# The sixth down step of the last two tiles by seven block products, new places for its left sides, and a third place for weight sums

## The chip, the cores and the metric

The kernel runs on one core of a Trainium2 chip. The time is that of one execution on the device in microseconds (us), and less is better. Five engines work side by side, each through its own queue in order: TensorE (PE, matrix products, with PEld for the loads of its stationary side), VectorE (DVE), ScalarE (ACT), GpSimd (POOL) and SyncE (SP), which here does nothing but issue transfers between the chip's two memories: the device memory, and the on-chip memory in which the engines read and write. An instruction at the head of a queue that waits for another engine or for a transfer holds up all that stands behind it in that queue.

## The reference: what is computed

An input `x` of 4096 rows by 640 columns goes through two blocks, each added to its input. The first is a spectral filter (Fourier transforms, a small network on the frequencies, and back); it is not touched. The second is a gated network:

```python
h = _layernorm(x, axis=-1) * (1 + cb) + sb
x = x + gb * ((_silu(h @ w_gate) * (h @ w_up)) @ w_down)
```

`w_gate` and `w_up` are 640 by 1728, `w_down` is 1728 by 640. The last product, here called the down product, is where the change lies. All of it is asked for in 32-bit precision. The kernel gets there with a faster number format of TensorE: each operand is split into a high and a low part, and a product is three matmuls (high by high, high by low, low by high).

## The kernel before, in words

The 4096 rows are worked as 32 blocks of 128 rows, in six tiles: tiles 0 and 1 of four blocks, tiles 2 to 5 of six. For each tile the 1728 inner columns come in chunks of 128, two chunks to a pair. A pair p (0 to 5) has a step for the gate (`g`), a step for `w_up` (`u`) and a down step. Behind the gate step of pair p+1 stands the down step of pair p; behind the sixth `u` step stands a step `m` (chunk 12, gate and up together), and then the sixth down step, which also takes chunk 12 and the half-filled chunk 13. The step `s`, early in the tile, makes chunk 13.

In tiles 2 to 5 the gate and up steps are done by Strassen's scheme in Winograd's form: a product of matrices of two by two blocks with seven block products instead of eight, from sums and differences of the blocks. The sums of weight blocks (`wt`) are made once in tiles 0 and 1, stored in the device memory (`td`) and loaded two per step in tiles 2 to 5 (line 2206). In each step PE makes seven products into four banks (lines 1887 to 1889, and 1898 to 1900 for the fifth block of rows), ACT copies four partial results out (`s_x`, `s_v`, `s_y`, `s_z`, line 1906), PE goes on adding into the same banks once the copy is made, and DVE adds copy and bank (line 1913).

The down product is plain in tiles 0 to 3 (`down`, line 2142, chunk 12 at line 2152): 11 matmuls of 320 columns for each of the tile's blocks and halves in a sixth step. In tiles 4 and 5 its first five steps are done by seven products too (`down7`, line 2056). This needs the seven blocks and sums of `w_down` per pair, split into high and low: `block_sums` (lines 1311 to 1350) loads four blocks (`B11` to `B22`), makes T1 to T4 on POOL, the high part on ACT (line 1328), the low part on DVE (line 1331), and stores them in `wsd` (line 1334); that runs beside tiles 1 and 2, and before tile 4 begins all of these stores must have been issued (the loop `until(("wst", p, x))`). `block_loads` brings them back. And it needs the left sides: `lefts` (line 1797) makes the products of gate and up (A11 to A22) and the sums S1 to S4 on POOL, and splits them on ACT (line 1816) and DVE (line 1819). In `down7` the seven products go into three groups of banks, X, Y and Z; X takes four of the seven products, with a DVE addition into the rows of `x` after each (line 2038); Z is copied by ACT and added by POOL.

In the sixth down step the weights of pairs 5 and 6 (6 is chunks 12 and 13) are loaded unsplit (`wdr`) and split in each tile by ACT (line 1373) and DVE (line 1377).

Beside the tile at hand runs the row work for the next one: the spectral result of each row block is finished, normed, transposed, and its left sides are split and stored (`hs<-ho`, lines 1465 to 1591), using the places `pc`, `px`, `h32` and `ho`.

The order of every queue is fixed when the program is built. A planner walks through the matmuls, keeps modelled times for each engine and each place (`room`), and puts a step of a chain into the queues when its inputs and places are free by that model (`tries`). What is needed and not yet placed is forced (`until`, `force`). The number of places per name stands in `bufs`: two for `wt`, two for `e` (where a split weight block waits for its store).

## Time and profile before

| what | value |
|---|---|
| median of 3 runs | 1481.1 us |
| the runs | 1473.35, 1481.52, 1481.1 us |
| profiled execution | 1476.28 us, of which the profile's span is 1474.4 us |
| PE busy | 1421.5 us, 96% |
| DVE, ACT, POOL busy | 1091.5, 805.4, 539.5 us |
| mean granted clock of TensorE | 0.996 |
| first matmul of tile 4 | 1083.9 us after the span's start |

The page gives the busy time of each engine and splits the span into 40 slices. From about 325 us on, when the gated network begins, PE is at nine tenths or more in every slice, and only the few microseconds in which it is not can be won without taking matmuls away. Busy times overlap: a matmul of 320 columns takes 312 ns from start to end, but the next starts some 147 ns after it.

### The profile page before, as it was taken

What the parts mean: (1) busy time and instruction counts of PE and PEld (TensorE: products, weight loads), DVE (VectorE), ACT (ScalarE), POOL (GpSimd) and SP (SyncE); (2) the same over time, 40 slices, a digit from 0 to 9 for tenths busy, and PEclk for the clock granted to TensorE, in tenths of its full rate; (3) what the DMA queues carried; (4) which work ended last, traced back from release to release, by engine and by line L of the source; (5) the groups of instructions that cost most, each with busy time, mean ns of one, the idle gap of its engine ahead of it and who ended that gap; (6) DMA issues with size and microseconds to landing.
All of it is one profiled execution on the core that took longest, in us unless ns stands there. A gap on an engine that the chain in (4) does not pass through costs nothing.

```text
span 1474.4 us, 24146 instructions
## 1 busy us (share of the span) xinstructions
PE 1421.5 (96%) x8646; PEld 1343.8 (91%) x8646; DVE 1091.5 (74%) x1979; ACT 805.4 (55%) x1594; POOL 539.5 (37%) x648
## 2 busy tenths in 40 slices
PE   6999999997999999999999999999999999999999
PEld 2799999975888888899999999999999999999998
DVE  8478888878788688848878857777747767467774
ACT  6578989845445565545565545555524435244432
POOL 5400110034564353412445422443324544046541
PEclk9999999999999999999999999999999999999999
DMA  9946555738767988798878995766796566965542
GB/s 376 334 166 182 157 187 163 221 104 273 256 246 236 367 290 273 271 390 293 276 271 264 319 373 189 260 223 205 268 363 205 202 209 206 374 196 208 202 156 100
DMA packets 171784, 363.21 MB, mean 246 GB/s; under 512 B 21457, under 2 KB 91537, under 8 KB 169617
## 3 DMA queue, kind: packets, MB, share of 16 engines
q1 hardware_dynamic: 163152, 344.14, 68.0%
q0 software_dynamic: 6928, 14.91, 3.2%
q10 hardware_dynamic: 1584, 2.62, 0.5%
q8 instruction: 68, 1.11, 0.3%
q14 instruction: 52, 0.42, 0.1%
HBM read 254.34 MB, written 98.11 MB: 239 GB/s over the span
## 4 chain that ended last, share of the span: by engine, by line
PE 70%; DVE 13%; DMA 8%; ACT 4%; issue 3%; POOL 1%; SPq 1%; DVEq 0%; ACTq 0%; POOLq 0%
PE pd L2142 16%; PE pw L1887 7%; PE pw L1888 7%; PE pw L1889 7%; PE pd_X L2056 4%; PE pc L657 2%; PE pg L1752 2%; PE pg L1753 2%; PE pg L1754 2%; PE pw L1898 2%; PE pw L1900 2%; PE pw L1899 2%; DVE wb L1222 2%; DMA wt<-td 2%; PE pd_Y L2056 2%
## 5 line engine op out<-in xcount | busy, mean ns | idle before, releaser
L2142 PE MATMUL pd<-wdh,a 128*128 128x320 f32 x1192 | 276.6, 312 | 2.0 <-DVE a L1789 1.8
L2142 PEld LDWEIGHTS pd<-wdh,a 128*128 128x128 f32 x1192 | 204.2, 190 | 3.0 <-DVE a L1789 2.1
L2142 PE MATMUL pd<-wdl,a 128*128 128x320 f32 x628 | 194.4, 311 | 0.0
L1222 DVE TENSOR_TENSOR wb<-r,wb 128x512 fp32r<-128x512 f32 (+3 forms) x156 | 161.8, 1043 | 21.1 <-ACT wb L1219 19.1
L2114 DVE TENSOR_TENSOR x<-x,pd 128x320 f32<-128x320 f32 x264 | 120.6, 479 | 55.1 <-PE pd L2142 50.3
L1887 PE MATMUL pw<-h,wt 128*128 128x384 f32 x416 | 140.5, 338 | 7.0 <-DMA wt<-td 5.2
L1888 PE MATMUL pw<-h,wt 128*128 128x384 f32 x416 | 139.2, 335 | 0.0
L1889 PE MATMUL pw<-h,wt 128*128 128x384 f32 x416 | 139.2, 335 | 0.0
L1219 ACT ACTIVATE wb<-r 128x512 fp32r<-128x512 f32 (+3 forms) x172 | 118.1, 703 | 32.9 <-PE pw L1900 22.7
L2142 PEld LDWEIGHTS pd<-wdl,a 128*128 128x128 f32 x628 | 119.0, 189 | 0.5
L1887 PE MATMUL pw<-h,wb 128*128 128x384 f32 x312 | 104.9, 336 | 0.0
L1889 PE MATMUL pw<-h,wb 128*128 128x384 f32 x312 | 104.7, 336 | 0.1
L1888 PE MATMUL pw<-h,wb 128*128 128x384 f32 x312 | 104.6, 335 | 0.0
L1752 PE MATMUL pg<-ht,wb 128*128 128x512 f32 x260 | 102.9, 396 | 1.2 <-ACT wb L1219 1.2
L1754 PE MATMUL pg<-ht,wb 128*128 128x512 f32 x260 | 101.8, 391 | 2.2 <-DVE wb L1222 2.2
L1753 PE MATMUL pg<-ht,wb 128*128 128x512 f32 x260 | 101.6, 391 | 0.0
L1465 POOL TENSOR_TENSOR cr<-cr,gab 128x640 f32<-128x640 f32 x28 | 46.9, 1676 | 126.8 <-DMA cr<-s 87.4
L1887 PEld LDWEIGHTS pw<-h,wt 128*128 128x128 f32 x416 | 78.1, 188 | 9.6 <-DMA wt<-td 5.1
L714 POOL DMA_DIRECT2D s<-co x28 | 15.5, 552 | 192.9 <-ACT co L713 186.1
L1906 ACT ACTIVATE s_x<-pw 128x384 f32<-128x384 f32 x52 | 25.4, 489 | 100.8 <-PE pw L1889 100.2
L1888 PEld LDWEIGHTS pw<-h,wt 128*128 128x128 f32 x416 | 78.2, 188 | 0.0
L1889 PEld LDWEIGHTS pw<-h,wt 128*128 128x128 f32 x416 | 78.2, 188 | 0.0
(315 smaller groups left out, 3977.7 us busy)
## 6 DMA issues: line engine op xcount, KB each, us to landing
wt<-td SPq DMA_DIRECT2D x104, 512.0 KB, 5.3
hs<-ho SPq DMA_DIRECT2D x52, 512.0 KB, 4.9
h<-hs SPq DMA_DIRECT2D x32, 768.0 KB, 7.6
r<-in_B_w_gate_dram SPq DMA_DIRECT2D x36, 640.0 KB, 5.6
r<-in_B_w_up_dram SPq DMA_DIRECT2D x36, 640.0 KB, 5.3
wdr<-wdd SPq DMA_DIRECT2D x25, 640.0 KB, 4.5
td<-wt SPq DMA_DIRECT2D x25, 512.0 KB, 5.9
g<-s SPq DMA_DIRECT2D x28, 320.0 KB, 7.8
```

What stands on the lines that cost most here:

```text
L1219: act.activation(wbs[t, n][:, 0, ks, e], raw[t, n][:, ks, e], AF.Copy)
L1222: (pool if onp else dve).tensor_tensor(wbs[t, n][:, 1, ks, e], raw[t, n][:, ks, e], f32(wbs[t, n][:, 0, ks, e]), op=OP.subtract)
L1465: pool.tensor_tensor(crs[r], crs[r], gab, op=OP.mult)
L1752: mm(b, wh, hh, start=(kk == 0), stop=False)
L1753: mm(b, wh, hl, start=False, stop=False)
L1754: mm(b, wl, hh, start=False, stop=(kk == 4))
L1887: mm(b, w(0, kp), a[:, kp, 0], start=start and kp == 0, stop=False, skip_group_check=not start)
L1888: mm(b, w(0, kp), a[:, kp, 1], start=False, stop=False, skip_group_check=not start)
L1889: mm(b, w(1, kp), a[:, kp, 0], start=False, stop=kp == 1, skip_group_check=not start)
L2056: mm(bk[b, i][:, :320], l[ln][:, x, c], w[wn, y], start=new and j == 0, stop=j == 2, skip_group_check=not new)
L2114: dve.tensor_tensor(x2[:, e], x2[:, e], x[0][:, :320], op=OP.add)
L2142: mm(pd[g, hf][0][:, :320], l, m, start=i == 0, stop=i == len(s) - 1 and not (last and len(gs) > 1))
```

## The change

1. The sixth down step of tiles 4 and 5 is done by seven products as well (`down7` with `last`). Chunks 12 and 13 are added to the Y, Z and X banks in plain form (5 matmuls), and to a fourth group of banks V. Z is here added by DVE like the others.
2. `block_sums` therefore runs for pair 5 (seven blocks) and for pair 6 (four blocks, only split, `TB`). The weights of pair 6 are loaded into `px` and `h32`, places that the row work has left. The splits of `wdr` go from tiles 4 and 5.
3. `e` has one place instead of two; the sources of the left sides now lie in `pc` instead of `m`, S2 and S3 in `ho` instead of `e`.
4. `wt` has three places, used in turn.

```diff
-            bufs = {"R": 2, "h1": 1, "wb": 2, "wt": 2, "wd": 1, "wdh": 2, "wdl": 2, "pc": 4, "px": 2, "gt": 2, "ho": 2,
-                    "h32": 1, "sg": 4, "s": 5, "gx": 2, "rb0": 1, "rb1": 1, "ra0": 1, "ra1": 1, "m": 5, "e": 2}
+            bufs = {"R": 2, "h1": 1, "wb": 2, "wt": 3, "wd": 1, "wdh": 2, "wdl": 2, "pc": 4, "px": 2, "gt": 2, "ho": 2,
+                    "h32": 1, "sg": 4, "s": 5, "gx": 2, "rb0": 1, "rb1": 1, "ra0": 1, "ra1": 1, "m": 5, "e": 1}
...
             def take(tag, shape, dt, bufs, name):
+                if tag == "wt":
+                    turns[0] += 1
+                    if turns[0] % 3 == 0:
+                        return low_p.tile(shape, dt, tag=tag, name=name)
+                    bufs = 2
...
+                if p == NPR:
+                    def tail(hl, f):
+                        w = wds.setdefault((t, p), {})
+                        if hl:
+                            w[hl, f] = take("px", [P, D], F32R, 2, f"tl{t}_{f}")
+                            nc.sync.dma_start(f32(w[hl, f]), wsd[p, :, 1, 2 * f:2 * f + 2])
+                        else:
+                            v = take("h32", [P, 2, D], F32R, 1, f"th{t}")
...
+            TB = ("B11", "B12", "B21", "B22")
...
-                for x in ("B22", "B21", "B11", "T3", "T1", "T2", "T4"):
+                bl = TB if p == NPR else ("B22", "B21", "B11", "T3", "T1", "T2", "T4")
+                for x in bl:
...
-                if t in DT and p < NPR - 1:
+                if t in DT:
                     return block_loads(t, p)
...
-            LT = {"A11": "a0", "A12": "a1", "S1": "a2", "A22": "a3", "S2": "e", "S3": "e", "S4": "wd"}
+            LT = {"A11": "a0", "A12": "a1", "S1": "a2", "A22": "a3", "S2": "ho", "S3": "ho", "S4": "wd"}
...
+                    for b, ln, wn, a, hf in (("X", "A11", "B11", 0, 0), ("Y", "S1", "T1", 1, 1), ("X", "S2", "T2", 0, 1),
+                                             ("X", "S3", "T3", 1, 1)):
+                        for i in range(H):
+                            put(b, i, prod(ln, wn, i))
+                            read(b, i, a, hf, False)
+                        if b == "Y":
+                            for a in range(2):
+                                until(("act", t, 12, a))
+                    for i in range(H):
+                        put("Y", i, prod("S4", "B22", i), (0, 1))
+                        read("Y", i, 0, 1, True)
+                    for i in range(H):
+                        put("Z", i, prod("A12", "B21", i), (0, 0))
+                        read("Z", i, 0, 0, True)
+                        out(0, i)
+                    for i in range(H):
+                        fin = t == NT - 1 and i == H - 1
+                        put("X", i, prod("A22", "T4", i), (1, 0))
+                        read("X", i, 1, 0, True)
...
+                        put("V", i, (), (1, 1))
+                        read("V", i, 1, 1, True)
...
             def down(t, p):
-                if t in DT and p < NPR - 1:
+                if t in DT:
                     return down7(t, p)
...
-            for p in range(NPR - 1):
+            for p in range(NPR + 1):
                 down_s.add(block_sums(p))
...
                 if t == min(DT):
-                    for p in range(NPR - 1):
-                        for x in BL:
+                    for p in range(NPR + 1):
+                        for x in TB if p == NPR else BL:
                             until(("wst", p, x))
```

Where the order of instructions moves, in rows of the two programs (line, operation, what is written and read, shape; `x2`, `x3` counts equal rows that follow each other; a name carries step and number).

SP at the end of tile 3 and the start of tile 4. The `out_dram` rows bring the finished rows of tile 3 out, `hs<-ho` are left sides of tile 5, `wt_10` and `wt_11` are weight sums of tile 4's second step, `x_4_0` and `x_4_1` the rows to which tile 4's first down step adds. Before:

```order
L2128 DMA out_dram<-x_3_0_10007 128x640 x3
L2128 DMA out_dram<-x_3_1_10087 128x640 x2
L1591 DMA hs<-ho_2_2_12401 128x2x512
L1303 DMA wdh_0_0_12435<-wsd 128x1280
L1591 DMA hs<-ho_2_3_12422 128x2x512
L1669 DMA x_4_0_12464<-x2d 128x1920
L2206 DMA wt_10_12475<-td 128x1024
L2206 DMA wt_11_12498<-td 128x1024
L2128 DMA out_dram<-x_3_1_10087 128x640
L1303 DMA wdl_0_0_12531<-wsd 128x1280
L1669 DMA x_4_1_12536<-x2d 128x1920
```

Of the change, first where tile 4 starts:

```order
L2220 DMA out_dram<-x_3_0_10045 128x640 x3
L2220 DMA out_dram<-x_3_1_10074 128x640 x2
L1616 DMA hs<-ho_2_2_12459 128x2x512
L1359 DMA wsd<-B12hl_12134 256x1x320
L1359 DMA wsd<-B21hl_12487 256x1x320
L1359 DMA wsd<-B22hl_12491 256x1x320
L2298 DMA wt_11_12576<-td 128x1024
L2298 DMA wt_30_12584<-td 128x1024
L1616 DMA hs<-ho_2_3_12480 128x2x512
```

and then, seven rows further, up to tile 4's first down step:

```order
L1208 DMA r_5_12720<-in_B_w_gate_dram 128x5x256
L1694 DMA x_4_0_12758<-x2d 128x1920
L2220 DMA out_dram<-x_3_1_10074 128x640
L2298 DMA wt_41_12797<-td 128x1024
L2298 DMA wt_50_12825<-td 128x1024
L1694 DMA x_4_1_12831<-x2d 128x1920
```

Three stores of pair 6's split blocks now stand at the start of tile 4, ahead of `wt_11`, `wt_30` and the last `hs`; `wt_10` went ahead into tile 3; the loads of `x_4_0` and `x_4_1` moved back behind the loads of the third gate step.

ACT at the same place, where `s_0_x` is the copy of tile 4's first product. Before:

```order
L1583 ACTIVATE ho_2_2_12401<-sa_2_0_12211 128x2x128 x2
L1583 ACTIVATE ho_2_3_12422<-sa_2_1_12212 128x2x128 x2
L1906 ACTIVATE s_0_x<-pw_0_0_12428 128x384
L1906 ACTIVATE s_0_v<-pw_0_3_12439 128x384
L1920 ACTIVATE sg_0_00_12460<-s_0_x 128x384
```

and of the change:

```order
L1608 ACTIVATE ho_2_2_12459<-sa_2_0_12269 128x2x128 x2
L1608 ACTIVATE ho_2_3_12480<-sa_2_1_12270 128x2x128 x2
L1353 ACTIVATE B21hl_12487<-B_6_12022 128x320
L1353 ACTIVATE B22hl_12491<-B_6_11997 128x320
L1932 ACTIVATE s_0_x<-pw_0_0_12495 128x384
L1932 ACTIVATE s_0_v<-pw_0_3_12504 128x384
L1932 ACTIVATE s_0_y<-pw_0_0_12495 128x384
```

Two splits of pair 6 now stand ahead of the first copy of tile 4; with one place `e`, each may start only when the store of the block before it has landed.

DVE at the start of tile 4's sixth down step. `s_13_z` and `s_13_v` are the last sums of step `m`, `a_13_..` the low parts of chunk 12, `wb_1` the low part of a weight of tile 5, and `pd_5_X`, `pd_5_Y` the banks. Of the change:

```order
L1939 TENSOR_TENSOR s_13_v<-pw_13_0_14291,s_13_v 128x384
L2068 TENSOR_TENSOR x_4_0_12758<-x_4_0_12758,pd_5_X_14413 128x320
L1229 TENSOR_TENSOR wb_1_14418<-r_1_14145,wb_1_14418 128x512
L2068 TENSOR_TENSOR x_4_0_12758<-x_4_0_12758,pd_5_X_14427 128x320
L2068 TENSOR_TENSOR x_4_0_12758<-x_4_0_12758,pd_5_X_14435 128x320
L2068 TENSOR_TENSOR x_4_1_12831<-x_4_1_12831,pd_5_Y_14440 128x320
L2068 TENSOR_TENSOR x_4_1_12831<-x_4_1_12831,pd_5_Y_14446 128x320
L2068 TENSOR_TENSOR x_4_1_12831<-x_4_1_12831,pd_5_Y_14451 128x320
L1963 TENSOR_TENSOR a_13_01_14407<-sg_13_00_14343,a_13_01_14407 128x384
L1963 TENSOR_TENSOR a_13_11_14412<-sg_13_10_14381,a_13_11_14412 128x384
L2068 TENSOR_TENSOR x_4_0_12758<-x_4_0_12758,pd_5_X_14413 128x320
L2068 TENSOR_TENSOR x_4_0_12758<-x_4_0_12758,pd_5_X_14427 128x320
```

Before, no bank of the down step was read there until chunk 12's matmuls were done; now six additions and half of `wb_1` stand ahead of `a_13_..`, and the second reading of X behind it.

More of the change, by code (lines that the diff above doesn't have):

```diff
@@ L2028, in read @@
                     q = bk[b, i]
-                    if b == "Z":
+                    if b == "Z" and not last:
                         hold("s")
@@ L2041, in read, with put @@
                         room[f"p{tags[b, i]}"].append(end)
[L2043 to L2045 removed]
+                    return end
+                def put(b, i, seq, tail=None):
+                    new = (b, i) not in bk
+                    if new:
+                        q = tags[b, i]
+                        wait_pe(hold(f"p{q}") - 0.1)
+                        bk[b, i] = bank(q, f"pd{t}_{p}_{b}{i}")
+                    seq = list(seq)
+                    if tail is not None:
+                        a, hf = tail
+                        for key in [("act", t, f, a) for f in (12, 13)]:
+                            until(key)
+                            wait_pe(done[key])
+                        v = wds[t, NPR]
+                        e = slice(320 * hf, 320 * hf + 320)
+                        g = H * a + i
+                        l12 = [left(t, 12, hl, g) for hl in range(2)]
+                        l13 = left(t, 13, 0, g)
+                        seq += [(l13, v[0, 1][:, e]), (l13, v[1, 1][:, e]),
+                                (l12[0], v[0, 0][:, e]), (l12[0], v[1, 0][:, e]), (l12[1], v[0, 0][:, e])]
+                    for j, (x, y) in enumerate(seq):
+                        mm(bk[b, i][:, :320], x, y, start=new and j == 0, stop=j == len(seq) - 1,
+                           skip_group_check=not new)
+                    slot(0.147 * len(seq))
@@ L2046, in down7, with prod @@
+                def prod(ln, wn, i):
                     until(("left", t, p, ln))
                     wait_pe(done["left", t, p, ln])
-                    for i in range(H):
-                        new = (b, i) not in bk
-                        if new:
-                            q = tags[b, i]
-                            wait_pe(hold(f"p{q}") - 0.1)
-                            bk[b, i] = bank(q, f"pd{t}_{p}_{b}{i}")
-                        c = slice(P * i, P * i + P)
-                        for j, (x, y) in enumerate(((0, 0), (0, 1), (1, 0))):
-                            mm(bk[b, i][:, :320], l[ln][:, x, c], w[wn, y], start=new and j == 0, stop=j == 2,
-                               skip_group_check=not new)
-                        slot(0.147 * 3)
-                        read(b, i, a, hf, (b, wn) in (("Z", "B21"), ("Y", "B22"), ("X", "T4")))
```

95 lines of the change are left out of this document (64 added, 31 removed).

## The prediction

> **What bounds the kernel now.** First the page: which engine is busy, and who waits for whom.
>
> ```profile
> PE 1421.5 (96%) x8646; PEld 1343.8 (91%) x8646; DVE 1091.5 (74%) x1979; ACT 805.4 (55%) x1594; POOL 539.5 (37%) x648
> PE   6999999997999999999999999999999999999999
> ```
>
> PE is the bound, and from the eleventh slice on without a visible hole. So an edit counts in two ways only: matmuls that it takes from PE, and stops of PE that it removes or makes. The stops are in the waits of PE, asked from 640 us (tile 2) to the end:
>
> ```profile
> PE pw L1887 <- DMA wt<-td: 5.2, 3, 3.1
> PE pw L1898 <- ACT s_z L1906: 4.0, 2, 3.0
> PE pw L1887 <- ACT s_x L1906: 1.7, 4, 0.6
> PE pd L2152 <- DVE a L1937: 0.6, 1, 0.6
> ```
>
> The columns are total, times, longest. About 11.5 us in all, 5.2 of them for weight sums. Tables by stretch say where (stretch, its length, busy time and count of PE, PEld, DVE, ACT and POOL, then the granted clock, the transfer engines' share and GB/s):
>
> ```profile
> 640.00:868.00 228.00, 222.37 (x1372) 220.38 (x1371) 175.73 (x310) 119.17 (x245) 90.64 (x106) 0.99 0.88 305
> 868.00:1084.00 216.00, 210.77 (x1307) 209.09 (x1306) 156.28 (x280) 109.84 (x223) 73.69 (x89) 1.00 0.73 251
> 1084.00:1277.00 193.00, 192.66 (x1181) 192.34 (x1180) 128.89 (x224) 83.62 (x171) 81.46 (x70) 1.00 0.69 242
> ```
>
> Tiles 2 and 3 lose 5 us each, tile 4 only 0.3. **Tile 4, where the new products lie, has hardly a stop to give; a stop there would be new.**
>
> **The matmuls taken away.** A sixth down step has 6 blocks x 2 halves x 11 = 132 matmuls; the new one 7 products x 3 blocks x 3 = 63, and 12 x 5 = 60 for chunks 12 and 13: 123. Nine fewer in each of two tiles.
>
> ```profile
> 1457.82 12.88 PE pd L2142 x88
> 1399.39 1.32 PE pd_Y L2056 x9
> ```
>
> 88 in 12.88 us and 9 in 1.32 us are both 0.147 us each: 18 x 0.147 = **-2.6 us**.
>
> **The third place for weight sums.** Three steps found a weight sum late, the longest wait (at 880 us) being that for `wt_10` in tile 3. With three places this load goes ahead into the tile before, and the later ones go ahead by a step. The next, `wt_11`, takes the place of `wt_00`, which comes free when `wt_10`'s old place did, and it is needed 21 matmuls later.
>
> ```profile
> 1087.34 0.34 PE L1900 MATMUL pw<-h,wb 128*128 128x384 f32 x1
> 1087.51 0.34 PE L1887 MATMUL pw<-h,wt 128*128 128x384 f32 x1
> wt<-td SPq DMA_DIRECT2D x104, 512.0 KB, 5.3
> ```
>
> One starts 0.17 us after the other, so that is 3.6 us more, against a longest wait of 3.1. I take the whole 5.2: **-5.2 us**, bounds -5.2 and 0 (SP holds it up elsewhere).
>
> **The start of tile 4: the new wait.** The split of pair 6 is not done when tile 4 begins; its last two blocks are forced in ahead of the first copy, and with one `e` each waits for the landing of the store before it. Rows for one turn, the store (issue to landing, least, median, most), the split's high part on ACT and its low part on DVE, in ns:
>
> ```profile
> DMA to landing us min/median/max: 2.6/3.9/8.3
> L1328 ACT ACTIVATE B21hl<-B x5: 453/471/472, 530.9 to 793.6; 128x320 fp32r<-128x320 f32 x5
> L1331 DVE TENSOR_TENSOR B21hl<-B,B21hl x5: 476/482/493, 534.0 to 794.1; 128x320 fp32r<-128x320 f32 x5
> ```
>
> and what stands there now on SP and on ACT (start, duration, and in brackets the idle time before it):
>
> ```profile
> 1082.03 0.38 SPq L1591 DMA_DIRECT2D hs<-ho  x1
> 1085.11 0.49 ACT L1906 ACTIVATE s_x<-pw 128x384 f32<-128x384 f32 x1 [2.36 <-PE pw L1889]
> ```
>
> B12's store is the next on SP after that `hs`: 1082.4. It lands at 1086.3; B21's high and low parts and SP's turn take 0.5 + 0.5 + 0.1, its store goes at 1087.4 and lands at 1091.3; B22's high part 0.5, then the copy 0.5: 1092.3. PE may go on adding in the first bank only then, and wants to at 1087.51, the second of the two matmuls shown above. A stop of 4.8 us. With 2.6 us for both stores it is 2.2, with 8.3 for both 13.6; I take the median, as no row of the three blocks lies far off it. Behind the stalled ACT stand only tile 4's copies, and behind the stalled SP `wt_11` and `wt_30`: `wt_11` would go at about 1093 and land 5.3 us later (the median above), and PE, itself late, asks for it at some 1103.
>
> A long stop costs more than itself. The only other one from ACT of that length, in tile 2, and the granted clock (the column before the DMA share) after it:
>
> ```profile
> 718.07 0.45 PE L1898 MATMUL pw<-h,wb 128*128 128x384 f32 x1 [2.97 <-ACT s_z L1906]
> 718.00:722.00 4.00, 3.93 (x15) 3.93 (x16) 3.14 (x7) 2.82 (x7) 0.00 (x0) 0.57 1.07 389
> 880.38 0.44 PE L1887 MATMUL pw<-h,wt 128*128 128x384 f32 x1 [3.10 <-DMA wt<-td]
> 880.00:884.00 4.00, 3.62 (x21) 3.62 (x22) 0.85 (x2) 2.20 (x5) 0.00 (x0) 1.00 0.92 376
> ```
>
> After 2.97 us idle the clock was 0.57 over 4 us, 0.43 x 4 = 1.7 us lost; after 3.10 us it was 1.00. So at about 3 us it can go either way, and at 4.8 I count it: 4.8 + 1.7 = **+6.5 us**. The Trainium skill ("TensorE: Matmul & The Clock Gate", section "HAM oscillation — how this bites in real kernels") wants no idle gap of PE above about 3.4 us; by that rule the 4.8 us stop would halve the clock too and the sum stays, and the trace agrees only in part, since one of the two gaps here lost the clock below that length.
>
> **The first down step of tile 4.** Here `x_4_1` is loaded behind `wt_50` on SP. That load takes the place of `wt_31`, which comes free when the gate step ahead of this down step has made its product T1.
>
> ```profile
> 1115.92 0.49 ACT L1906 ACTIVATE s_z<-pw 128x384 f32<-128x384 f32 x1 [0.37 <-PE pw L1889]
> x<-x2d SPq DMA_DIRECT2D x8, 960.0 KB, 8.8
> 1121.92 1.32 PE pd_Y L2056 x9
> 1124.57 1.32 PE pd_Y L2056 x9
> ```
>
> The copy of T1 at 1115.9 marks it. Two SP issues later, at 1116.4, `x_4_1` goes; with 8.8 us it lands at 1125.2, the first addition from Y ends 0.5 us later, and PE wants to add to Y again at 1124.57 (the first Y row is when it filled it). All of this is shifted alike by the stop before. **+1.2 us**; a load of 5.6 us, the least of that line, gives 0, one of 10.7 gives 3.1. The cover before was large: the load stood at the tile's start.
>
> **The sixth down step itself.** Its first twelve groups of three matmuls are each followed by a DVE addition into the rows, and X comes twice running (S2, S3). PE fills X0 for S3 at 27 matmuls, 3.96 us, after the step's start, if DVE has read it.
>
> ```profile
> 1257.83 4.69 PE pd L2142 x32
> 1257.87 0.55 DVE L1913 TENSOR_TENSOR s_v<-pw,s_v 128x384 f32<-128x384 f32 x1
> 1261.28 1.02 DVE L1937 TENSOR_TENSOR a<-sg,a 128x384 fp32r<-128x384 f32 x2
> 1399.87 1.37 DVE L2038 TENSOR_TENSOR x<-x,pd_Y 128x320 f32<-128x320 f32 x3
> 1401.19 1.37 DVE L2038 TENSOR_TENSOR x<-x,pd_X 128x320 f32<-128x320 f32 x3
> L1222 DVE TENSOR_TENSOR wb<-r,wb 128x512 fp32r<-128x512 f32 x36 | 34.0, 946 | 0.8 <-ACT wb L1219 0.4
> ```
>
> DVE's queue from the step's start (1257.83): `s_v` till 0.6; X0, half a microsecond, till 1.1; half a `wb`, 946 ns on average, till 2.0; five additions, of which three take 1.32 us from one row to the next, 0.44 each, till 4.2; the two low parts of chunk 12, 1.0, till 5.3; X0 again till 5.8. PE waits 5.8 - 4.0 = 1.8 us in tile 4. In tile 5 there is no `wb`: 0.9 less, 0.9 us. **+2.7 us**, bounds 0.5 (the low parts early) and 4. Later groups have eight matmuls (1.2 us) to each addition. The removed splits of `wdr` (ACT and DVE) lay beside PE's work and give nothing: the list of PE's waits has no row for `wdl`. The end of the kernel stays: the last addition, then two short stores.
>
> **Tiles 1 to 3 with one `e`.** Eleven more blocks are split (11 x 0.46 us on ACT, 11 x 0.48 on DVE, four subtractions on POOL, 19 transfers), beside PE. That alone is hidden: by the stretches above ACT is busy for 229 of 444 us there, DVE for 332. But each of some 33 splits in tiles 2 and 3 now stands behind the store of the one before. The planner allows 0.45 + 0.9 + 0.9 + 0.9 = 3.15 us for it (an issue, a start, the transfer, its end, in `run`); the store's median is 3.9. So ACT stands 0.75 us longer on average, 25 us in all. Before, with two places:
>
> ```profile
> DMA wsd<-T1hl: 0.4, 1
> DMA wsd<-B11hl: 0.4, 1
> ```
>
> 0.8 us in all. How much comes through to PE? After a copy `s_y` or `s_z` PE has nine matmuls, 1.6 us, before it adds again, and the copy takes 0.5: a good half of all waits finds slack. I estimate a sixth, **+4 us**. Bounds: -4, if the two stops for `s_z` above (both with a split T1 just ahead of the copy) go with the new order, and +13, half of it.
>
> **The sum.** -2.6 - 5.2 + 6.5 + 1.2 + 2.7 + 4 = +6.6 us. On the profiled execution, 1476.3 us (its span and 1.9 us around it), that is 1483. This execution is 4.8 us below the median of the runs, 1481.1, inside their spread; the four executions that are known average 1478.1. I set the forecast on that: **1485 us**.
>
> **Rivals.**
> - *Short stores* (0.20). At the start of tile 4 both stores land near 2.6 us, since SP has sent fewer loads just before: a stop of 2.2, too short for the clock, the terms of the two down steps come out at 0.6 and 2, and the two `s_z` stops go: 1478.1 - 2.6 - 5.2 + 2.2 + 0.6 + 2 - 4 = **1471**. For it: the least of 2.6 occurs for B21. Against: half of the stores took more than 3.9. The Trainium skill ("DMA: Bandwidth & Descriptors", "Anatomy of one DMA") fits 2.0 us and 436 bytes per ns for one DMA of the GpSimd queue; by it a 320 KB store would take an estimated 2.75 us, and the stop would be 2.5 us. It speaks for this rival; the median of 3.9 us speaks against.
> - *One `e` starves ACT* (0.22), the case on the other side. The waits for stores fall on copies. It decides from 1.1 us on, the slack of an `s_y` or `s_z` copy; at half of 25 us it is +13 and three more drops of the clock, 5: 1478.1 + 2.6 + 13 + 5 = **1499**, where 2.6 is the sum without its last term. For it: 2.97 us of idle came from one late copy. Against: DVE and ACT have free time in which the planner puts the splits.
> - *The third place doesn't help* (0.10). SP is late with everything at a tile's start, so `wt_11` is what is late: the 5.2 stays, **1490**. Against: `wt_11` has 3.6 us more.
>
> **How the numbers follow.** Forecast 0.48, rivals 0.20, 0.22, 0.10. A measurement of this kernel can't tell less than about 1%, 15 us, from no change. Slower by more than that needs 1496 and up: most of the second rival and a fifteenth of the rest, 0.20. Faster by more than that, below 1466, needs all gains and no new wait, 0.04. Within: 0.76. The range leaves out the ends of the store's and the `e` bounds: 1467 to 1502; the likeliest case alone, 1476 to 1494.
>
> **What would show it.** In the profile after: ACT's B21 and B22 splits start about 1086 and 1091, waiting for `wsd<-B12hl` and `wsd<-B21hl`, and PE idle some 5 us at the first T2 of tile 4, with the clock below 1 behind it; no wait for `wt<-td` above 1 us; a wait of PE for DVE's `x` in both sixth down steps, before X of S3; ACT waiting for `wsd` in tiles 2 and 3 some 25 us. The forecast is wrong if tile 4's start has no stop, or if tiles 2 and 3 grow by more than 10 us.

## The result and the profile after

The changed kernel takes 1485.6 us (median of 12 runs, 1483.1 to 1488.8), the kernel before 1477.6 us in the same session (12 runs, 1472.8 to 1482.9). The ratio is **1.0052, 95% interval 1.0034 to 1.0070**: half a per cent slower, some 8 us, and so within 1%. The forecast was 1485 us. Two of its terms were wrong by some 4 us each, in opposite directions, and the experiments below are mostly about those two.

The profiled execution of the changed kernel has a span of 1482.2 us, 7.8 us more than before. The page first: busy time of PE, and the granted clock in 40 slices.

```profile
PE 1422.3 (96%) x8628; PEld 1344.2 (91%) x8628; DVE 1103.4 (74%) x2012; ACT 809.7 (55%) x1603; POOL 548.1 (37%) x660
PEclk9999999999999999999999999999989999999999
```

PE has 18 matmuls fewer, as counted, and still 0.8 us more busy time: one slice, the thirtieth, has a lower clock. The larger waits of PE from tile 2 to the end (total, times, longest; three of 0.6 us and less are left out):

```profile
PE pw L1913 <- ACT s_x L1932: 8.3, 4, 6.1
PE pw L1924 <- ACT s_z L1932: 5.6, 4, 3.7
PE pd_X L2094 <- DVE x L2068: 1.9, 2, 1.4
PE py L1507 <- ACT chh L1494: 0.9, 1, 0.9
PE pr L2030 <- DVE wb L1229: 0.8, 1, 0.8
```

No wait for weight sums (`wt<-td`) is left, 5.2 us before. New are, above all, one wait of 6.1 us for `s_x` and two for DVE's additions into `x`. Where in the kernel the 7.8 us lie is read from the first matmul of tiles 2, 4 and 5, in the trace of before

```profile
647.41 0.34 PE L1887 MATMUL pw<-h,wb 128*128 128x384 f32 x1
1083.87 0.34 PE L1887 MATMUL pw<-h,wb 128*128 128x384 f32 x1
1276.98 0.34 PE L1887 MATMUL pw<-h,wb 128*128 128x384 f32 x1
```

and in that of after:

```profile
645.52 0.34 PE L1913 MATMUL pw<-h,wb 128*128 128x384 f32 x1
1080.81 0.34 PE L1913 MATMUL pw<-h,wb 128*128 128x384 f32 x1
1285.61 0.34 PE L1913 MATMUL pw<-h,wb 128*128 128x384 f32 x1
```

| stretch | before | after | difference | forecast for it |
|---|---|---|---|---|
| up to tile 2 | 647.4 | 645.5 | -1.9 | 0 |
| tiles 2 and 3 | 436.5 | 435.3 | -1.2 | -1.2 (third place -5.2, one `e` +4) |
| tile 4 | 193.1 | 204.8 | +11.7 | +8.2 (start 6.5, down steps 1.2 and 1.8, matmuls -1.3) |
| tile 5 to the end | 197.4 | 196.6 | -0.8 | -0.4 |

The whole loss is in tile 4, and nearly all of it at its start. On ACT and on SP stand there, in the changed kernel (start, duration, idle time before it and what ended it):

```profile
1086.16 0.47 ACT L1353 ACTIVATE B21hl<-B 128x320 fp32r<-128x320 f32 x1 [6.35 <-DMA wsd<-B12hl]
1089.85 0.47 ACT L1353 ACTIVATE B22hl<-B 128x320 fp32r<-128x320 f32 x1 [3.22 <-DMA wsd<-B21hl]
1090.22 0.47 ACT L1932 ACTIVATE s_x<-pw 128x384 f32<-128x384 f32 x1
```

```profile
1079.50 0.53 SPq L1359 DMA_DIRECT2D wsd<-B12hl  x1
1087.18 0.52 SPq L1359 DMA_DIRECT2D wsd<-B21hl  x1
```

The two forced splits stand ahead of the first copy, each behind the landing of the store before it, as the forecast had it. From issue to release the first store took 6.7 us (1079.50 to 1086.16), the second 2.7 (1087.18 to the end of ACT's idle time at 1089.85); the forecast took 3.9 for each. PE meanwhile, and two stretches of 4 us behind it (the granted clock is the column before the DMA share):

```profile
1090.75 0.69 PE L1913 MATMUL pw<-h,wt 128*128 128x384 f32 x1 [6.13 <-ACT s_x L1932]
```

```profile
1092.00:1096.00 4.00, 4.00 (x14) 4.00 (x13) 0.00 (x0) 0.49 (x1) 0.00 (x0) 0.50 0.64 213
1096.00:1100.00 4.00, 4.00 (x22) 4.00 (x22) 1.43 (x3) 0.49 (x1) 0.00 (x0) 0.90 0.39 76
```

PE stands for 6.1 us, not 4.8, and then runs at 0.50 from 1090.75 to 1096 and at 0.90 on average over the next 4 us: 5.25 x 0.5 + 4 x 0.1 = 3.0 us lost, not 1.7. The Trainium skill ("TensorE: Matmul & The Clock Gate", section "HAM oscillation — how this bites in real kernels") says that PE gaps above about 3.4 us take the clock to half; after this gap the trace agrees, with 0.50.

### The profile page after: what moved, and what is told of

It is laid out like the page before. It is cut to its first block, busy times and chain, and to the rows that moved or that the text cites. A ratio compares the mean times of both kernels' runs of the same rounds, so it can differ in the third digit from the quotient of the medians.

```text
span 1482.2 us, 24216 instructions
## 1 busy us (share of the span) xinstructions
PE 1422.3 (96%) x8628; PEld 1344.2 (91%) x8628; DVE 1103.4 (74%) x2012; ACT 809.7 (55%) x1603; POOL 548.1 (37%) x660
## 4 chain that ended last, share of the span: by engine, by line
PE 65%; DVE 14%; DMA 10%; ACT 6%; issue 3%; SPq 2%; POOL 1%; DVEq 0%; ACTq 0%; POOLq 0%
PE pd L2234 11%; PE pw L1913 7%; PE pw L1915 7%; PE pw L1914 7%; PE pd_X L2094 4%; DVE wb L1229 2%; PE pd_Y L2094 2%; PE pg L1778 2%; PE pg L1777 2%; PE pg L1779 2%; PE pw L1924 2%; PE pw L1926 2%; PE pw L1925 2%; PE pc L657 2%; DMA hs<-ho 2%
## 5 line engine op out<-in xcount | busy, mean ns | idle before, releaser
L2234 PE MATMUL pd<-wdh,a 128*128 128x320 f32 x1040 | 239.8, 311 | 1.6 <-DVE a L1814 1.1
L2234 PEld LDWEIGHTS pd<-wdh,a 128*128 128x128 f32 x1040 | 177.1, 189 | 2.5 <-DVE a L1814 1.3
L1229 DVE TENSOR_TENSOR wb<-r,wb 128x512 fp32r<-128x512 f32 (+3 forms) x156 | 168.1, 1087 | 13.5 <-ACT wb L1226 11.9
L2234 PE MATMUL pd<-wdl,a 128*128 128x320 f32 x540 | 166.8, 310 | 0.0
L1913 PE MATMUL pw<-h,wt 128*128 128x384 f32 x416 | 142.0, 341 | 8.6 <-ACT s_x L1932 8.3
L1914 PE MATMUL pw<-h,wt 128*128 128x384 f32 x416 | 140.7, 338 | 0.0
L1915 PE MATMUL pw<-h,wt 128*128 128x384 f32 x416 | 140.7, 338 | 0.0
L2206 DVE TENSOR_TENSOR x<-x,pd 128x320 f32<-128x320 f32 x240 | 109.2, 478 | 35.9 <-PE pd L2234 31.7
L2234 PEld LDWEIGHTS pd<-wdl,a 128*128 128x128 f32 x540 | 101.8, 189 | 0.5
L1913 PEld LDWEIGHTS pw<-h,wt 128*128 128x128 f32 x416 | 78.9, 190 | 10.5 <-ACT s_x L1932 9.5
```

What stands on the lines that cost most here:

```text
L1229: (pool if onp else dve).tensor_tensor(wbs[t, n][:, 1, ks, e], raw[t, n][:, ks, e], f32(wbs[t, n][:, 0, ks, e]), op=OP.subtract)
L1913: mm(b, w(0, kp), a[:, kp, 0], start=start and kp == 0, stop=False, skip_group_check=not start)
L1914: mm(b, w(0, kp), a[:, kp, 1], start=False, stop=False, skip_group_check=not start)
L1915: mm(b, w(1, kp), a[:, kp, 0], start=False, stop=kp == 1, skip_group_check=not start)
L2206: dve.tensor_tensor(x2[:, e], x2[:, e], x[0][:, :320], op=OP.add)
L2234: mm(pd[g, hf][0][:, :320], l, m, start=i == 0, stop=i == len(s) - 1 and not (last and len(gs) > 1))
```

## The experiments

All times are medians, all ratios against the kernel before, run beside it. The medians of the kernel before lay between 1477.6 and 1480.3 us in the different sessions, so kernels of different rows are compared by ratios and by the stops in their traces.

| kernel | sixth step | places `wt` | places `e` | median us | ratio, 95% interval |
|---|---|---|---|---|---|
| changed kernel | seven products | 3 | 1 | 1485.6 | 1.0052, 1.0034 to 1.0070 |
| e1_not_forced | seven products | 3 | 1 | 1476.1 | 0.9962, 0.9944 to 0.9979 |
| e2_wt_two | seven products | 2 | 1 | 1484.1 | 1.0021, 1.0001 to 1.0040 |
| e3_wt_two_e_two | seven products | 2 | 2 | 1482.4 | 1.0006, 0.9987 to 1.0025 |
| e4_plain_sixth | plain | 3 | 1 | 1475.0 | 0.9952, 0.9932 to 0.9973 |
| e5_z_between | seven, Z earlier | 3 | 1 | 1474.4 | 0.9960, 0.9942 to 0.9978 |
| e6_plain_sixth_wt_two | plain | 2 | 1 | 1483.2 | 1.0032, 1.0014 to 1.0051 |
| e7_sums_on_dve | as e1 | 3 | 1 | 1473.4 | 0.9970, 0.9953 to 0.9988 |
| e8_wt_two_again | seven products | 2 | 1 | 1483.1 | 1.0032, 1.0015 to 1.0048 |
| e9_spare_place | as e8 | 2 and a spare | 1 | 1478.6 | 0.9994, 0.9978 to 1.0011 |
| e10_plain_spare | as e6 | 2 and a spare | 1 | 1477.5 | 0.9995, 0.9979 to 1.0012 |
| e11_all_three | as e5 and e7 | 3 | 1 | 1473.3 | 0.9950, 0.9933 to 0.9968 |
| e12_left_sums_on_dve | as e11 | 3 | 1 | 1463.3 | 0.9894, 0.9869 to 0.9919 |

### The forced wait at tile 4's start

```diff
-                    for p in range(NPR + 1):
-                        for x in TB if p == NPR else BL:
+                    for p in range(NPR):
+                        for x in BL:
                             until(("wst", p, x))
```

> Only the loop ahead of tile 4 is changed: it no longer forces the stores of pair 6, so the last two splits of pair 6 (B21, B22) stand some 30 us later, one by one, where the planner puts them. In the changed kernel's trace the stop at the start of tile 4 is 6.3 us, the clock is at 0.5 to 0.9 for about 8 us behind it, and two small stops (1.0 and 1.0 us) follow where before had 0 and 0.5. Theory (this forced wait is the whole loss): tile 4's start loses nothing, about 10 us come back, 1475 us, 2 to 3 us under the kernel before. Rival (the wait only moves: each split still stands behind the landing of the store before it, with ACT's copies behind it): a stop of about 2 us or two near 30 us into tile 4, too short for the clock, 1478 to 1480 us.

Measured: 1476.1 us, ratio 0.9962. All that PE waits for in tile 4 (1081 to 1275 us):

```profile
PE pd_X L2094 <- DVE x L2068: 1.4, 1, 1.4
PE pw L1913 <- ACT s_x L1932: 0.3, 1, 0.3
```

The stop is gone and none has come in its place: the two splits, some 30 us later, find gaps of ACT. The theory holds. The wait cost 9.4 us by the medians and 0.9%, 13 us, by the ratios; the trace of the changed kernel gives 6.1 + 3.0 for stop and clock, and 1.4 for two later stops that e1 doesn't have (0.8 for `pr`, 0.6 more for an `s_x`): 10.5 us. The two profiles agree with that: tile 4 takes 204.8 us in the changed kernel and 194.0 in e1, 10.8 less. So without the forced splits the change would have been a gain of 0.4%.

### The third place for weight sums, and one place `e`

The first two of these kernels take the third place back, and the second gives `e` its second place again:

```diff
-            bufs = {"R": 2, "h1": 1, "wb": 2, "wt": 3, "wd": 1, "wdh": 2, "wdl": 2, "pc": 4, "px": 2, "gt": 2, "ho": 2,
+            bufs = {"R": 2, "h1": 1, "wb": 2, "wt": 2, "wd": 1, "wdh": 2, "wdl": 2, "pc": 4, "px": 2, "gt": 2, "ho": 2,
...
-                    if turns[0] % 3 == 0:
+                    if False:
                         return low_p.tile(shape, dt, tag=tag, name=name)
```

> The changed kernel with two places for weight sums, all else kept. Theory (the third place is worth the waits for weight sums that the trace of before shows, 5.2 us): 1485.5 + 5.2 = 1491 us, and waits of PE for wt<-td of about 5 us in all are back. Rival (the third place takes away waits that other late work would take the place of): 1485 to 1487 us, with the waits for wt<-td back but others smaller.

> The changed kernel with two places for weight sums and two for split weight blocks; left are the sixth down step by seven products and the left sides in their new places. All splits of pair 6 are then made in tile 3, so nothing is forced at tile 4's start. Theory (18 matmuls less, -2.6, and the stops in both sixth down steps, 1.58 and 0.67 in the changed kernel's trace, +2.25): the kernel before less 0.4, 1477 us; no wait of ACT for wsd above 1 us, no stop at the start of tile 4. Rival (the stop at tile 4's start comes from the output stores and row work on SP, not from the one place): a stop of 3 us or more there, and 1481 or more.

Measured: 1484.1 us (1.0021), where 1491 was expected, and 1482.4 us (1.0006). Neither stops at the start of tile 4. In e3 that was expected; in e2 it was not: there the order of the steps came out so that pair 6 was split in tile 3. So e2 has to be held against e1, which has no such stop either, and then the third place is worth 8 us by the medians. For e3, the kernel before less 0.4 us was expected and its ratio is 1.0006 (-2 to +4 us): the sixth step by seven products with its new places, and nothing else, changes nothing that can be told. ACT's waits for stores are down to 1.5 us in tiles 2 and 3 there (the longest 1.1), about as expected.

The fourth kernel of that session is the kernel before with the new places alone (`pc` and `ho` for the left sides, one `e`, three `wt`), its sixth step plain:

> The kernel before with the new places alone (left sides in pc and ho, one place e, three places for weight sums); the sixth down step is plain as before, so pair 6 isn't split. Theory (third place -5.2; one e in tiles 2 and 3 for 28 blocks in place of 39, +3): 1475.5 us, no stop at tile 4's start. Rival 1 (one e costs nothing; the stop of 3.8 us in tile 2 of the changed kernel is DVE beside POOL's unbroken work): 1472 us. Rival 2 (one e starves ACT even with 28 blocks): 1480 or more, with ACT waiting for wsd more than 10 us in tiles 2 and 3.

Measured: 1475.0 us, ratio 0.9952. ACT waits 6.7 us for stores in tiles 2 and 3. It lies where the theory put it, but this could be -5.2 + 3 or something else. Two more kernels were to show the size of the third place: e4 and e1 with two of them.

> As e4_plain_sixth, but with two places for weight sums: the kernel before with its left sides moved and one place e, nothing else. Theory (third place -5 us; one e costs a few us): 1480 to 1482, that is 5 to 7 over e4_plain_sixth (1475.0) and 1 to 3 over the kernel before. Rival (the third place gives only what the trace of e2_wt_two shows in tiles 2 and 3, 2.7 us): 1477.7 us.

> As e1_not_forced with two places for weight sums; beside e2_wt_two only one store (B22 of pair 6) stands 18 us later. The trace of e2_wt_two lost 5 to 7 us in tile 0, where its program is that of the changed kernel, and 2.7 us more than e1_not_forced in tiles 2 and 3. Theory (the third place is worth its waits, 3 to 5 us; tile 0 is chance): 1479 to 1481 us. Rival (the median of e2_wt_two stands: third place worth 8 us): 1484 us, with tile 0 slow again.

Measured: 1483.2 us and 1483.1 us, both 1.0032. So 7 to 8 us again, although PE's waits for weight sums are 3.4 us in e8. The rest is not in tiles 2 and 3 at all, but in tile 0, where these kernels have the same program as e1. In e8 between 322 and 340 us (ACT, then PE):

```profile
ACT hx L1729 <- DMA s<-cz: 3.7, 1, 3.7
```

```profile
PE pg L1739 <- DVE ht L1730: 4.4, 1, 4.4
```

All three kernels with two `wt` and one `e` have this wait of ACT, none of the others. What differs there is only where the places lie in the on-chip memory. The next two kernels set the third place aside without using it; the instructions of every engine and their order stay as in e8 and e6:

```diff
-                    if False:
-                        return low_p.tile(shape, dt, tag=tag, name=name)
+                    if turns[0] == 3:
+                        low_p.tile(shape, dt, tag=tag, name="spare")
```

> As e8_wt_two_again (1483.1 us), with the same instructions in the same order on every engine; the memory of the third place for weight sums is set aside and never used, so that all other places lie where they lie in e1_not_forced. In the traces of the three runs with two places for weight sums and one place e, ACT waits 3.5 to 3.7 us in tile 0 for a transfer (s<-cz) before hx, which no other run has, and PE stops 4.5 us there in place of 1.2 to 1.8. Theory (that wait comes from hx lying where cz lay; the third place by itself is worth the waits for weight sums, 3 to 5 us): no such wait of ACT, 1479 to 1480 us. Rival (the place does nothing for tile 0): the wait stays, 1483 us.

> As e6_plain_sixth_wt_two (1483.2 us), same instructions, same order, the third place set aside and unused. Against the kernel before it has one place e for two and the left sides in other places, nothing else; against e4_plain_sixth (1475.0 us) it has the third place unused. Theory: about 1479 us, so that one e costs next to nothing against the kernel before (0 to 2 us) and the third place gives 4 us. Rival (one e costs the 4 us of the prediction): 1482 to 1483 us, the third place gives 7 to 8.

Measured: 1478.6 us (0.9994) and 1477.5 us (0.9995). ACT's wait before `hx` is gone, and in e9 PE waits at the same place

```profile
PE pg L1739 <- DVE ht L1730: 1.5, 1, 1.5
```

and the other kernels 1.0 to 1.6. So 4.5 and 5.7 us of the 8, by the medians, were a matter of addresses, and the first theory on e2 and e8 (tile 0 is chance) fell: it was there in three runs of three. That `hx` lies where `cz` lay is an inference from the wait; the addresses themselves were not looked at. Nor is it shown that this one wait is all of the difference: up to tile 2 the profiled execution of e9 is only 0.3 us shorter than that of e8 (649.8 against 650.2 us), that of e10 11.5 us shorter than that of e6 (642.5 against 654.0). (Tile 0 has holes in every kernel: in the page of before PE is at seven tenths in the tenth slice, 332 to 369 us, so that nine tenths in every slice hold from there on, not from 325 us.)

Without that wait, two differences can be read. e10 against the kernel before, whose addresses are not alike but which doesn't have the wait either: one place `e` and the left sides' new places cost -0.05% (-3 to +2 us), **nothing**. And with the addresses alike, e1 against e9 and e4 against e10: the third place is worth 0.32 and 0.43%, 4.7 and 6.4 us, by the ratios, 2.5 us by the medians. PE's waits for weight sums in e9 lie between:

```profile
PE pw L1913 <- DMA wt<-td: 3.8, 3, 2.0
```

### The sixth down step

In e5, on top of e1, two of Z's products go between the second and the third X:

```diff
                     for b, ln, wn, a, hf in (("X", "A11", "B11", 0, 0), ("Y", "S1", "T1", 1, 1), ("X", "S2", "T2", 0, 1),
                                              ("X", "S3", "T3", 1, 1)):
+                        if ln == "S3":
+                            for i in range(2):
+                                put("Z", i, prod("A12", "B21", i))
                         for i in range(H):
...
-                        put("Z", i, prod("A12", "B21", i), (0, 0))
+                        put("Z", i, prod("A12", "B21", i) if i > 1 else (), (0, 0))
```

> As e1_not_forced, and in both sixth down steps the first two of the three products of Z (A12 by B21) are done between X S2 and X S3, their matmuls for chunks 12 and 13 later, in their old place. PE then comes to X S3 six matmuls, 0.88 us, later, while DVE works off the additions and low parts ahead of the read of X S2. Theory (DVE's queue is what PE waits for at X S3): the stops of 1.57 and 0.67 us in e1_not_forced become 0.7 and 0, 1.5 us less, 1474.5 us. Rival (the delay moves on with PE, because the forced low parts go behind later additions): stops as before, 1476 us.

Measured: 1474.4 us, ratio 0.9960. In both sixth down steps together (1255 to 1475 us) PE now waits for DVE's additions

```profile
PE pd_X L2094 <- DVE x L2068: 0.5, 1, 0.5
```

once, 0.5 us idle; e1 had 1.9 us in two. The mechanism is as the theory says. The 1.5 us themselves can't be told from e1 by the times (0.9960 against 0.9962). Nor can the gain of the whole step: e1 (0.9962) and e4 (0.9952) differ in nothing but the sixth step and the splits that it needs, and what is left of the 18 matmuls saved (2.6 us) after the stops of 1.9 us is too little to be told.

### The stop in tile 2

The changed kernel has its longest stop before tile 4 at 806 us, for a copy `s_z`; all the kernels with one `e` have it too, e12 aside (2.8 to 3.7 us). The forecast would lay it to the one `e`. DVE and POOL just before, in the changed kernel:

```profile
798.74 4.21 DVE L1229 TENSOR_TENSOR wb<-r,wb 128x512 fp32r<-128x512 f32 x1 [0.53 <-ACT wb L1226]
802.88 1.98 DVE L1612 TENSOR_TENSOR ho<-h,ho 128x256 fp32r<-128x256 f32 x2
804.78 1.92 DVE L1963 TENSOR_TENSOR a<-sg,a 128x384 fp32r<-128x384 f32 x1
806.63 0.54 DVE L1939 TENSOR_TENSOR s_x<-pw,s_x 128x384 f32<-128x384 f32 x1
```

```profile
797.67 0.73 POOL L1592 TENSOR_TENSOR sa<-h 128x256 f32<-128x256 f32 x1 [2.33 <-ACT h L1575]
798.35 0.64 POOL L1482 DMA_DIRECT2D gt<-in_k_ga_dram  x1
799.02 1.02 POOL L1960 TENSOR_TENSOR sg<-s_z,sg 128x384 f32<-128x384 f32 x1
800.00 1.01 POOL L1960 TENSOR_TENSOR sg<-s_v,sg 128x384 f32<-128x384 f32 x1
800.98 0.73 POOL L1592 TENSOR_TENSOR sa<-h 128x256 f32<-128x256 f32 x1
801.67 0.73 POOL L1592 TENSOR_TENSOR sa<-sa,h 128x256 f32<-128x256 f32 x1
802.48 1.07 POOL L1592 TENSOR_TENSOR sa<-h,sa 128x256 f32<-128x256 f32 x1
803.52 1.05 POOL L1349 TENSOR_TENSOR T<-B,B 128x320 f32<-128x320 f32 x1
```

The split `wb` of 128x512, on average 0.98 us in this kernel, takes 4.21; the low part `a`, 0.55 elsewhere, takes 1.92. POOL, which at 798.35 issues a transfer, has no gap of more than 0.03 us between its rows from 797.67 until 802.40. `s_x` comes so late on DVE that ACT, waiting for it, has not yet copied `s_z`. Two kernels take work from POOL. In e7, on top of e1, the sums of down-weight blocks go to DVE:

```diff
-                    pool.tensor_tensor(src[x], src[a], src[b], op=OP.subtract)
+                    dve.tensor_tensor(src[x], src[a], src[b], op=OP.subtract)
...
-                        out.append(Step("P", 0.95, lambda x=x: sub(x), (k("tv", a), k("tv", b)), k("tv", x),
+                        out.append(Step("V", 0.5, lambda x=x: sub(x), (k("tv", a), k("tv", b)), k("tv", x),
```

> As e1_not_forced, with the 24 subtractions of down-weight blocks (T1 to T4 of six pairs) on DVE in place of POOL, 0.5 us each. The stop of 3.85 us in tile 2 (at 806 us in the changed kernel, PE waiting for a copy s_z, ACT for DVE) stands behind one DVE split wb of 4.2 us beside POOL's unbroken work from 799 to 807 us, of which two such subtractions are 2.2 us. Theory (POOL's unbroken work slows DVE): less POOL work, no DVE wb above 3 us there and a stop under 2 us; 1474 us, or 1476 if DVE's 12 us more cost it elsewhere. Rival (the stop comes from ACT's wait for the one e): 3 us or more stay.

Measured: 1473.4 us, ratio 0.9970, no different from e1. The expectation failed in its numbers: the `wb` takes 4.22 us as before,

```profile
799.97 4.22 DVE L1229 TENSOR_TENSOR wb<-r,wb 128x512 fp32r<-128x512 f32 x1 [0.53 <-ACT wb L1226]
```

since the sums that were moved stand behind it, not beside it; the stop is 2.8 us in place of 3.7. e11 puts this and e5's edit together:

> e1_not_forced with both changes that helped: two products of Z between X S2 and X S3 (1.5 us less PE stops) and the subtractions of down-weight blocks on DVE (2 to 3 us less by e7_sums_on_dve). Theory (the two are far apart in the kernel and add): 1472 us, 0.994 of the kernel before or less. Rival (DVE's 12 us more make it late in the sixth down step of tile 4, or a gain of e7 was chance): 1474 to 1475 us.

Measured: 1473.3 us, ratio 0.9950: better than the kernel before, but short of the 0.994 expected, and not distinguishable from e1 (0.9962). In e12 the three `sa` rows that do stand beside the `wb` go to DVE as well:

```diff
-                    pool.tensor_tensor(o, a, b, op=op)
+                    dve.tensor_tensor(o, a, b, op=op)
...
-                sm = [Step("P", 0.76, lambda j=j: sum_l(j), sd[j], k("S", j), ("pc", "pc") if j == 0 else ()) for j in range(4)]
+                sm = [Step("V", 0.42, lambda j=j: sum_l(j), sd[j], k("S", j), ("pc", "pc") if j == 0 else ()) for j in range(4)]
```

> As e11_all_three (1473.3 us), and the sums of the row work's left sides (sa, 48 of 128x256) on DVE too, 0.42 us each, in place of POOL's 0.74. In tile 2 of all kernels with one place e, one DVE split wb of 128x512 takes 4.2 us, in place of some 0.9, beside five POOL instructions without a gap between them, of which three are these sums; ACT waits for DVE behind it and PE stops 3 to 3.9 us for a copy s_z. Theory (what slows DVE is POOL's work without a gap): that wb takes 2.5 us or less, the stop for s_z in tile 2 is under 1.5 us, 1470 to 1471 us. Rival (the wb is slow for another reason, transfers into its memory for one): it stays above 3.5 us and the stop with it, 1473 to 1475 us.

Measured: **1463.3 us, ratio 0.9894** (0.9869 to 0.9919), 10 us under e11 by the medians, 8 by the ratios, the fastest of all, and some 7 us better than the theory had it. The `wb` at that place, and what is left of PE's waits in tiles 2 and 3:

```profile
799.44 0.76 DVE L1229 TENSOR_TENSOR wb<-r,wb 128x512 fp32r<-128x512 f32 x1 [0.20 <-ACT wb L1226]
```

```profile
PE py L1507 <- DVE chl L1497: 0.9, 2, 0.4
PE pw L1913 <- ACT s_x L1932: 0.7, 1, 0.7
PE pw L1924 <- ACT s_z L1932: 0.2, 1, 0.2
```

The waits for `s_z`, 4.7 us in e11, are 0.2, and with them go the drops of the clock. DVE has 72 instructions more than in the changed kernel (24 from e7's edit, 48 from this one) and is busy for only 4 us more, 1107.7 us; POOL is down from 548.1 to 488.7:

```profile
PE 1419.7 (97%) x8628; PEld 1342.9 (92%) x8628; DVE 1107.7 (76%) x2084; ACT 809.5 (55%) x1603; POOL 488.7 (33%) x588
```

The gain of e12 over e11 lies in tiles 2 and 3 alone: by the first matmuls of the tiles they take 426.0 us in e12 and 436.7 in e11, the rest differs by less than 1 us either way. In e11 the stop behind the slow `wb` is 2.8 us, and the clock is 0.50 for 6.0 us behind it, 3.0 us lost: 5.8 of the 10.7. PE's other waits there fell from 5.8 to 1.8 us; whether that is POOL's lighter load or the other order that e12's steps came to stand in stays open.

So the stop goes when POOL has less work beside that `wb`, with the one `e` kept: the one `e` by itself is not its cause. The kernel before, with two, has a slow split as well, 3.38 us for 128x768 at 808.75 beside POOL's rows, without a stop of PE behind it. That it is the missing gap on POOL that holds DVE is not shown. In e12 two rows of POOL stand beside the `wb` without a gap too (798.60 and 799.61), and it takes its usual time. And the slow splits of the changed kernel and of the kernel before both began while POOL was issuing a transfer (798.35 and 808.36, 0.64 us each), which in e12 stands at 795.67, away from the `wb`; no kernel moved that issue alone.

## Why the prediction was right, and where it was not

The total, 1485 against 1485.6, came out right, and its largest cause, the forced wait at tile 4's start, is the true one (e1). That it fits to a microsecond is luck: the start of tile 4 was priced 4 us too low, the one `e` 4 us too high, and the two down steps 2 us too high together. With these put right the sum would be 4.6 us, against 7.8 between the two profiles; most of the rest lies in tiles 2 and 3, where 5.2 us of waits for weight sums went and only 1.2 us were gained. The prediction also held that less than 1% can't be told from no change; twelve runs of each kernel gave an interval of 0.2% to either side. Step by step:

- **The matmuls taken away, -2.6.** Right: 8646 became 8628.
- **The third place, -5.2.** Right in mechanism and about in size: no `wt<-td` wait is left, and e1 against e9, e4 against e10 give 2.5 to 6.4 us.
- **The start of tile 4, +6.5.** The mechanism was right row by row: `B21` at 1086, `B22` at 1090, released by the two stores named, PE stopped at the first T2. (The times themselves were met by luck: tile 4 began 3.1 us earlier, and B12's store took 2.8 us longer.) The term was too small; it measured 10.5. The two stores took 6.66 and 2.67, together 9.3 us, where twice the median was 7.8, and the stop was 6.1 in place of 4.8; the clock went to 0.50 for 5 us where the row of tile 2 (0.57 for 4 us) was taken as its price, 3.0 in place of 1.7; and 1.4 us of stops behind it, with ACT and SP late, were not in the sum at all. The sentence that only tile 4's copies stand behind the stalled ACT was the error there: weight splits `wb` stood there too, and `pr` of the step `s` waited for one.
- **The first down step of tile 4, +1.2.** Wrong, it was 0. `x_4_1` does go late, behind the weight sum, and DVE does wait for it:

```profile
1131.31 1.28 DVE L2068 TENSOR_TENSOR x<-x,pd_Y 128x320 f32<-128x320 f32 x3 [0.98 <-DMA x<-x2d]
```

  but the load, issued at 1125.94, took 5.4 us, not the line's median of 8.8, and PE, which wanted that bank again at 1132.3, did not notice. The lower bound was the truth.
- **The sixth down step, +2.7.** Right in mechanism and somewhat large: 1.42 and 0.51 us idle, 1.9 in all, and the queue of DVE in tile 4 as it was written down, read of X, half a `wb`, five additions, two low parts, read of X:

```profile
1266.79 0.47 DVE L2068 TENSOR_TENSOR x<-x,pd_X 128x320 f32<-128x320 f32 x1
1267.18 0.87 DVE L1229 TENSOR_TENSOR wb<-r,wb 128x512 fp32r<-128x512 f32 x1
1267.98 0.87 DVE L2068 TENSOR_TENSOR x<-x,pd_X 128x320 f32<-128x320 f32 x2
1268.77 1.27 DVE L2068 TENSOR_TENSOR x<-x,pd_Y 128x320 f32<-128x320 f32 x3
1269.96 1.01 DVE L1963 TENSOR_TENSOR a<-sg,a 128x384 fp32r<-128x384 f32 x2
1270.90 1.27 DVE L2068 TENSOR_TENSOR x<-x,pd_X 128x320 f32<-128x320 f32 x3
```

```profile
1271.43 0.41 PE L2094 MATMUL pd_X<-wdh,lS 128*128 128x320 f32 x1 [1.42 <-DVE x L2068]
```

- **Tiles 1 to 3 with one `e`, +4.** Wrong: e10 puts it at nothing (-3 to +2) with the 28 blocks of the plain kernel, and with pair 6's eleven more e1 can't be told from e4. The 25 us of ACT's waits were 9.5,

```profile
ACT T3hl L1353 <- DMA wsd<-B11hl: 3.7, 2, 2.3
ACT T1hl L1353 <- DMA wsd<-T3hl: 2.4, 2, 1.3
ACT B21hl L1353 <- DMA wsd<-B22hl: 1.9, 1, 1.9
ACT T2hl L1353 <- DMA wsd<-T1hl: 1.5, 2, 1.1
```

  and what of them reached PE can't be told from none. Multiplying the mean lateness of a store by the number of splits took every split as due the moment its place should be free; the planner seldom puts one there so soon. The stretch still came out as forecast, -1.2, but partly by luck: other stops, for POOL's and DVE's sake, stood in this term's place.

Of the rivals, *one `e` starves ACT* is refuted by e10, *the third place doesn't help* by e1 against e9, and *short stores* by the trace: of the two stores that count, one was short and one long. The profiles up to tile 2 differ by 1.9 us more, with no row of the change to explain it; the 12 runs of the kernel before spread over 10 us, so that much may be chance, or come from the moved places.

## What to carry to other kernels

A place whose release is the landing of a transfer cost nothing here while the planner chose when to fill it, and the full landing, the clock behind it and what queues up behind that as soon as one line of code forced it ahead of a copy that PE needed; look for such forced lines first. When an instruction on DVE takes several times its usual time, look at what POOL does beside it before laying the stop to the change at hand; here moving small sums from the less busy engine to the busier one gave 0.56% by the ratios (e12 against e11), more than the whole change without its forced wait (0.38%, e1). And when the number of places is changed, keep the addresses of the others (a spare, unused place does it), or the comparison measures them too.

## What the runs showed of the hardware that was not expected

- DVE beside POOL. A 128x512 split takes 4.2 us beside POOL's rows in tile 2, in every kernel with one `e` but e12, and 0.98 us on average. In the rows above it began while POOL was issuing a transfer, 0.28 us before the next of POOL's sums, and ended 0.55 us after the first gap on POOL (802.40). The Trainium skill ("SBUF — State Buffer", section "🔬 SBUF: two separate sides") has the two engines share a pair of ports as an exclusive lock, which the one that starts first holds for its whole instruction. The trace agrees in that one engine stands while the other keeps its usual time; not in that the wait ends with one instruction: DVE let four of POOL's sums pass. In e12 it was the other way round: the split took 0.76 us, and POOL's sum beside it 1.46 in place of 1.01. What decides between the two is open.
- The clock. Over the 4 us behind an idle time of PE of only 2.33 us it was 0.57 (e10_plain_spare, the matmul and the 4 us),

```profile
730.64 0.45 PE L1895 MATMUL pw<-h,wt 128*128 128x384 f32 x1 [2.33 <-ACT s_y L1914]
```

```profile
730.60:734.60 4.00, 3.96 (x14) 3.96 (x15) 2.37 (x6) 1.64 (x3) 3.36 (x6) 0.57 0.48 158
```

  while it stayed at 1.00 after 2.65 us in e6_plain_sixth_wt_two, and after the 3.10 us of the prediction. So between 2.3 and 3.1 us the length of the gap doesn't decide it alone; what does is open. Cut finer, these means are made of 0.50 and 1.00 only, and the stretches at 0.50 have few lengths: 3.4 us in e10 (731.1 to 734.5), 6.8 in e11 (811.4 to 818.2), 10.2 behind the 6.13 us stop of the changed kernel (1086.6 to 1096.8).
- Addresses. With the same instructions in the same order, the position of the places alone moved the time by 4.5 us (e8 and e9) and 5.7 us (e6 and e10).
